# Token numbers inside the sorted rows, a fixed GpSimd issue order, and smaller edits in a fused attention and expert kernel

## The chip, the cores and the metric

The kernel runs on one core of a Trainium2 chip. Its time is the device time of one execution in microseconds (us), taken by the chip. A profiled execution also leaves a trace: what each engine did and when. The engines are PE (matrix products), DVE (vector), ACT (activation functions), POOL (GpSimd) and SP, which here only issues transfers. POOL issues the transfers that convert float32 to float16 and those that scatter rows to places given by an index list.

## The reference

Attention over 8 batches, 8 heads, 576 tokens and 64 columns a head, with a bias that a small two-layer network (MLP) computes from the distance of two tokens; then every token goes through the one expert, of eight, that its domain number names.

```python
scores = scale * np.matmul(q, k.transpose(0, 1, 3, 2))
psi_rel = np.log1p(np.abs(rel))                       # rel = i - j
psi_i = np.log1p(np.maximum(pos[:, None], 1.0))
h = np.maximum((psi_rel / psi_i)[..., None] @ w1 + b1, 0.0)   # 32 hidden
scores = scores + (h @ w2).transpose(2, 0, 1)[None]
attn = softmax(scores); x = attn @ v                  # -> x: 4608 tokens x 512
for e in range(8):
    mask = domain_id == e
    out[mask] = np.maximum(x[mask] @ w1[e], 0.0) @ w2[e]      # 512 -> 1024 -> 512
```

## The kernel before, in words

The program runs through these stages. PE, DVE and ACT execute in the order in which the code is written; on POOL and SP a scheduler of the compiler chooses the order.

**Setup** (L63 to L108). Number tables are made on POOL by sixteen iota instructions, four for each quarter of the partitions, and turned into two tables: L4 (logarithms of distances, 1711 columns) and slope (144 columns).

**Bias** (L111 to L164). Nine blocks `ib` of 64 queries. For each, 16 tiles `hr` (128 x 576, the hidden layer) are made on DVE (L126), PE multiplies them with W2BIG into PSUM tiles `eb` (L136, L141), and ACT writes the exponentials out as biasM, biasR, biasL and biasRL (L150 to L164). The last 64 keys are computed twice, once for each half of the partitions (L140).

**Zero fill**. x_dram (`fire_x`), 9984 rows of 512 float16, is filled with zeros by one transfer on SP (L694). On the same queue the second part of the domain numbers, `dom2` (L183), stands behind it.

**Route** (L167 to L292). DVE counts the tokens of each expert and computes `posi`, the row of each token in sorted order; one count goes through PE (`app`, L207), which stands behind the last bias product in PE's order. Then a second table in DRAM, `fire_perm`, is filled with a pad number, 40 scatters on POOL (L287, one for each column of 128 or 64 tokens) write every token's number of 4 bytes to its row, and one transfer on SP reads the table back as `sidx` (L292).

**Attention** (L295 to L536). For each batch: the loads of q, k and v on POOL (two batches ahead), transposes on PE, then 21 units of scores. A unit is two or more products on PE into `sc`, an exponential on ACT (L412, `e`), and a product with the bias on DVE (L417). The products with v (`av`) are spread between later units; `norm` (L454 to L473) divides by the row sums, and five scatters a batch on POOL (L477) send 4 x 128 and 64 rows of 1 KB to x_dram. For the last 64 queries the product with v runs on 64 columns of one head at a time (L439, L444) and `norm` writes the tile `xl`.

**Experts** (L547 to L614). x_dram is read back by SP, 640 rows for an expert (`xg`, L578), transposed on PE (L559), multiplied with w1e (L601), through a Relu on ACT (L605), multiplied with w2e (L566); DVE copies 128 rows at a time from PSUM to `res` (L569, four buffers), and POOL scatters these rows to the output by `sidx` (L570). The weights of experts 0 to 2 are loaded early into three buffers, those of 3 to 6 all at the start of this stage (L591 to L593), those of 7 when a buffer comes free.

Of the kernel before, what the change touches and what calls it, by code (L numbers as in the profile page):

```python
# [16 lines left out]
P = 128  # L17
S = 576
# [12 lines left out]
PAD = 1 << 20  # L31

# [23 lines left out]
def _no_order(tc, key, inst):  # L56

    ins = inst.ins if hasattr(inst, "ins") else inst
    tc.declare_no_dep(ins, group=key, reason="rows of one permutation")
    tc.add_to_no_dep_group(key, ins)  # L60


def _setup_constants(tc, G, w1, b1, w2):  # L63
# [12 lines left out]
    nc.sync.dma_start(out=w1col, in_=bass.AP(tensor=w1.tensor, offset=0, ap=[[0, 4], [1, 32], [1, 1]]))  # L76
    G.nb1 = cst.tile([P, 1], F32, tag="nb1", name="nb1")
    nc.sync.dma_start(out=G.nb1, in_=bass.AP(tensor=b1.tensor, offset=0, ap=[[0, 4], [1, 32], [1, 1]]))
    nc.vector.tensor_scalar(out=G.nb1, in0=G.nb1, scalar1=-1.0, scalar2=None, op0=AO.mult)
# [9 lines left out]
    si = cst.tile([P, NGR], I32, tag="si", name="si")  # L89
    li = G.tmp.tile([P, W4 + W1], I32, tag="li", name="li")  # L90
    for g in range(4):
        pg = slice(32 * g, 32 * g + 32)

        nc.gpsimd.iota(si[pg, 0:128], base=4 * g, channel_multiplier=0, pattern=[[1, 4], [16, 32]])
        nc.gpsimd.iota(si[pg, 128:144], base=512 + g, channel_multiplier=0, pattern=[[4, 16]])
        nc.gpsimd.iota(li[pg, 0:W4], base=-(C4 + 4 * g), channel_multiplier=0, pattern=[[1, W4]])
        nc.gpsimd.iota(li[pg, W4:], base=-(C1 + 512 + g), channel_multiplier=0, pattern=[[1, W1]])
    G.slope = cst.tile([P, NGR], F32, tag="slope", name="slope")
    nc.vector.tensor_copy(out=G.slope, in_=si)
    nc.vector.tensor_scalar(out=G.slope, in0=G.slope, scalar1=1.0, scalar2=None, op0=AO.max)  # L100
    nc.scalar.activation(out=G.slope, in_=G.slope, func=AF.Ln, bias=1.0, scale=1.0)
    nc.vector.reciprocal(out=G.slope, in_=G.slope)
    nc.vector.tensor_scalar(out=G.slope, in0=G.slope, scalar1=w1col[:], scalar2=None, op0=AO.mult)
    lf = G.tmp.tile([P, W4 + W1], F32, tag="lf", name="lf")
    nc.vector.tensor_copy(out=lf, in_=li)
# [190 lines left out]
class _Attention:  # L296
# [152 lines left out]
    def norm(self, b, p):  # L449
# [5 lines left out]
        if p < 4:  # L455
            if p == 0:
                self.xt[b] = asb.tile([P, 4, 512], F16, tag="xt", name="xt", bufs=2)
# [282 lines left out]
```

## Time and profile before

| | us |
|---|---|
| median of 3 runs | 527.84 |
| lowest, highest | 526.59, 532.48 |
| the profiled execution | 523.68 |
| its span in the trace | 522.0 |
| busy: PE, DVE, ACT, POOL | 373.6, 260.3, 231.1, 202.0 |

The span is what the trace covers; 1.7 us of the execution lie around it. No engine is busy for the whole span, so what bounds the kernel changes from stage to stage and is read stage by stage. In a line of the timeline the first number is the start, the second the length, and the bracket tells how long the engine had been idle and what ended that.

### The profile page before, as it was taken

The page shows a single profiled execution, that of the slowest core. Times are in us where ns is not written, and L with a number is a line of the kernel's source. Part 1 is how long each engine was busy: PE and PEld are TensorE (multiplying, and loading weights), DVE is VectorE, ACT ScalarE, POOL GpSimd, SP SyncE. Part 2 cuts the span into 40 slices and gives each one's busy share as a digit, 9 for nine tenths or more (in the row PEclk, how much of TensorE's full clock was granted, in tenths as well). Part 3 has the DMA queues.
Part 4 walks back from the last instruction along what each step waited for, and adds up shares of the span by engine and source line. Part 5 has one row for each costly group of instructions (what it writes and reads, how often), then busy time and mean ns, then how long its engine had stood idle before and what let it go on. Part 6 is the DMA issues. An engine that isn't in the chain of part 4 may idle for free. (4 is left out here: it accounts for less than half of the span.)

```text
span 522.0 us, 10886 instructions
## 1 busy us (share of the span) xinstructions
PE 373.6 (72%) x4578; PEld 235.3 (45%) x4578; DVE 260.3 (50%) x572; ACT 231.1 (44%) x290; POOL 202.0 (39%) x238
## 2 busy tenths in 40 slices
PE   0578844311298988889898977079639999999992
PEld 0366733100055555465555544055425566566550
DVE  5899985100369695777768674013022422422411
ACT  1444521000388987889697875021402143143140
POOL 9740445777606546543403042603013303313312
PEclk9999999555599999999897989579959999999997
DMA  0999987000992999979401010899998313102211
GB/s 3 155 233 366 319 123 131 2 0 0 99 155 53 161 203 149 151 124 114 77 3 46 4 46 21 160 241 241 215 246 206 112 50 123 69 22 88 81 39 73
DMA packets 79034, 61.39 MB, mean 118 GB/s; under 512 B 23558, under 2 KB 71430, under 8 KB 78984
## 3 DMA queue, kind: packets, MB, share of 16 engines
q0 software_dynamic: 56576, 45.12, 49.7%
q1 hardware_dynamic: 22408, 15.57, 10.8%
q8 instruction: 36, 0.59, 0.4%
q14 instruction: 14, 0.11, 0.1%
HBM read 67.17 MB, written 25.49 MB: 177 GB/s over the span
## 5 line engine op out<-in xcount | busy, mean ns | idle before, releaser
L412 ACT ACTIVATE e<-sc 128x1024 f16<-128x1024 f32 x168 | 156.7, 998 | 93.5 <-remote 67.2
L605 ACT ACTIVATE hT<-hps 128x640 f16<-128x640 f32 x64 | 45.1, 704 | 137.8 <-PE hps L601 136.2
L570 POOL DMA_INDIRECT out_dram<-res,sidx x40 | 39.5, 988 | 132.6 <-DVE res L569 131.9
L566 PE MATMUL ops<-w2e,hT 128*128 128x512 f16 x320 | 71.5, 383 | 0.0
L601 PE MATMUL hps<-xT,w1e 128*128 128x320 f16 x512 | 71.2, 300 | 0.0
L385 PE MATMUL sc<-qkT 64*128 64x512 f16 x256 | 54.3, 407 | 22.7 <-ACT e L412 16.7
L477 POOL DMA_INDIRECT fire_x<-xt,posi x32 | 34.4, 1076 | 81.2 <-DVE xt L459 71.0
L569 DVE COPY res<-ops 128x512 f32<-128x512 f32 x40 | 27.7, 691 | 76.2 <-PE ops L566 51.0
L417 DVE TENSOR_TENSOR e<-e,biasM 128x1024 f16<-128x1024 f16 x96 | 63.4, 685 | 3.3 <-ACT e L412 3.0
L601 PEld LDWEIGHTS <-w1e 128*128 128x128 f16 x512 | 50.3, 98 | 20.7
L136 PE MATMUL eb<-W2BIG,hr 128*128 128x32 f16 x576 | 36.0, 196 | 25.8 <-DVE hr L126 18.8
L433 PE MATMUL pu<-vext,e 128*128 128x65 f16 x1024 | 53.0, 199 | 0.0
L126 DVE TENSOR_SCALAR hr<-L,slope,nb 128x576 f16<-128x576 f16 x144 | 51.6, 435 | 1.7 <-ACT L L108 1.7
L561 DVE COPY xT<-pxt 128x512 f16<-128x512 f16 x40 | 15.8, 421 | 65.8 <-PE pxt L559 64.1
L566 PEld LDWEIGHTS <-hT 128*128 128x128 f16 x320 | 31.3, 99 | 36.8 <-issue 1.4
L287 POOL DMA_INDIRECT fire_perm<-nidx,posi x40 | 38.7, 969 | 21.0 <-issue 21.0
L433 PEld LDWEIGHTS <-e 128*128 128x128 f16 x1024 | 46.2, 102 | 0.0
L367 DVE COPY qkT<-pt 128x1024 f16<-128x1024 f16 x32 | 21.8, 683 | 47.7 <-remote 43.5
L136 PEld LDWEIGHTS <-hr 128*128 128x128 f16 x576 | 26.5, 117 | 34.7 <-DVE hr L126 17.6
L429 PE MATMUL pu<-vrag,e 128*128 128x130 f16 x128 | 29.9, 234 | 13.1 <-DVE xl L470 7.9
L559 PE MATMUL pxt<-idn,xg 128*128 128x128 f16 x160 | 15.1, 235 | 33.6 <-DMA xg<-fire_x 18.1
L345 PE MATMUL pt<-idn,qn 128*64 128x128 f16 x256 | 15.3, 249 | 27.1 <-DVE qkT L367 14.3
(123 smaller groups left out, 407.6 us busy)
## 6 DMA issues: line engine op xcount, KB each, us to landing
fire_x<-zero SPq DMA_DIRECT2D x1, 9984.0 KB, 37.0
w1e<-in_moe_w_dram POOLq DMA_DIRECT2D x8, 1024.0 KB
w2e<-in_moe_w_dram POOLq DMA_DIRECT2D x8, 1024.0 KB
xg<-fire_x SPq DMA_DIRECT2D x8, 640.0 KB, 8.6
qn<-in_q_dram POOLq DMA_DIRECT2D x8, 512.0 KB
kn<-in_k_dram POOLq DMA_DIRECT2D x8, 512.0 KB
vst<-in_v_dram POOLq DMA_DIRECT2D x8, 512.0 KB
fire_perm<-nidx,posi POOLq DMA_INDIRECT x40
```

The source lines that it names most:

```text
L126: nc.vector.tensor_scalar(out=hr, in0=G.L4[:, c0: c0 + S], scalar1=G.slope[:, m: m + 1], scalar2=G.nb1[:], op0=AO.mult, op1=AO.max)
L136: nc.tensor.matmul(out=eb[:, lj, 32 * k16: 32 * k16 + 32], lhsT=rap(hr, jc, [[4, 128]]), rhs=G.W2BIG[:, 0:32], start=True, stop=True)
L287: _no_order(tc, "slots", nc.gpsimd.indirect_dma_start(out=G.perm_dram[:, :], out_offset=bass.IndirectOffsetOnAxis(ap=G.posi[0:n, c:c + 1], ...
L385: mm(out=sc[:, h2, :], lhsT=self.qkT[b, p][hs[h2], 1, 128 * c: 128 * c + 128], rhs=self.qkT[b, p][hs[h2], 0, :], start=not raw, stop=True)
L412: nc.scalar.activation(out=ef[:, 0:n], in_=sf[:, 0:n], func=AF.Exp, bias=0.0, scale=0.125)
L417: self.nc.vector.tensor_tensor(out=job[0], in0=job[0], in1=job[1], op=AO.mult)
L433: mm(out=self.pu[:, c // 2, o + 65 * h2: o + 65 * h2 + 65], lhsT=self.e[b, ("m", p, j)][:, h2, 128 * c: 128 * c + 128], rhs=vx[:, 2 * p + ...
L477: _no_order(self.tc, "x_rows", self.nc.gpsimd.indirect_dma_start(out=self.x_dram[:, :], out_offset=bass.IndirectOffsetOnAxis(ap=self.G.pos ...
L566: nc.tensor.matmul(out=ops_, lhsT=hT[:, fc, t0: t0 + 128], rhs=w2e[:, fc, :], start=(fc == 0), stop=(fc == 7))
L570: _no_order(tc, "out_rows", nc.gpsimd.indirect_dma_start(out=out[:], out_offset=bass.IndirectOffsetOnAxis(ap=idx, axis=0), in_=res[:], in_ ...
L601: nc.tensor.matmul(out=hps[:, hf, 0:HC], lhsT=w1e[:, dc, 128 * fc: 128 * fc + 128], rhs=xT[:, dc, HC * hf: HC * hf + HC], start=(dc == 0), ...
L605: nc.scalar.activation(out=hT[:, fc, :].rearrange("p (a b) -> p a b", a=2), in_=hps[:, :, 0:HC], func=AF.Relu, bias=0.0, scale=1.0)
```

## The change

1. **Token numbers.** A row of x_dram grows from 512 to 514 float16 (`XW = DM + 2`, 1028 bytes): the last two hold the token's number as one int32. It is written into `xt` and `xl` by a small iota on POOL (`new_rows`), travels with the scatter of the rows, comes back with `xg`, and is the index of the output scatter. The table fire_perm, its pad transfer, its 40 scatters and `sidx` are gone. The pad number is written by the zero fill.
2. **Order on POOL.** An `_Issue` object puts each load, iota and weight load behind the one before it; scatters between two such instructions are free among themselves.
3. **Fetches of rows**: one transfer of 128 rows instead of 640, two experts ahead instead of three. **Weights** of expert e + 3 are issued behind the first output scatter of expert e. `res` has six buffers.
4. **Last queries**: 128 columns, two heads at once, in `av`; `norm` of `xl` in two pieces, `norm` of `xt` in one instruction instead of two.
5. **Bias**: of 16 hidden tiles, three (3, 8, 13) are made on ACT; the last keys are multiplied once; the setup has fewer and wider iotas, and a chain of small DVE operations and two absolute values on ACT in their place.

```diff
+XW = DM + 2
+class _Issue:
+    def __init__(self, tc):
+        self.tc, self.fixed, self.free = tc, None, []
+    def _behind(self, ins, before):
+        self.tc.add_manual_dep(ins, before.name, mybir.DependencyInfo(
+            mybir.DependencyClass.NoSync, mybir.DependencyReason.DATA), reason="issue order")
+    def __call__(self, inst):
+        ins = _ins(inst)
+        for before in self.free or ([self.fixed] if self.fixed is not None else []):
+            self._behind(ins, before)
+        self.fixed, self.free = ins, []
+        return inst
+    def scatter(self, inst):
+        ins = _ins(inst)
+        if self.fixed is not None:
+            self._behind(ins, self.fixed)
+        self.free.append(ins)
+        return inst
...
-                nc.vector.tensor_scalar(out=hr, in0=G.L4[:, c0: c0 + S],
-                                        scalar1=G.slope[:, m: m + 1], scalar2=G.nb1[:],
-                                        op0=AO.mult, op1=AO.max)
+                if k16 in (3, 8, 13):
+                    nc.scalar.activation(out=hr, in_=G.L4[:, c0: c0 + S], func=AF.Relu,
+                                         bias=G.pb1[:], scale=G.slope[:, m: m + 1])
+                else:
+                    nc.vector.tensor_scalar(out=hr, in0=G.L4[:, c0: c0 + S],
+                                            scalar1=G.slope[:, m: m + 1], scalar2=G.nb1[:],
+                                            op0=AO.mult, op1=AO.max)
...
-    for bb in range(B):
-        for t in range(NT):
-            n = 128 if t < 4 else 64
-            c = NT * bb + t
-            _no_order(tc, "slots", nc.gpsimd.indirect_dma_start(
-                out=G.perm_dram[:, :],
-                out_offset=bass.IndirectOffsetOnAxis(ap=G.posi[0:n, c:c + 1], axis=0),
-                in_=nidx[0:n, bb, t:t + 1], in_offset=None))
-    G.sidx = pbuf.tile([P, E * NCH, 1], I32, tag="sidx", name="sidx")
-    nc.sync.dma_start(out=G.sidx, in_=bass.AP(tensor=G.perm_dram.tensor, offset=0,
-                                              ap=[[1, 128], [128, E * NCH], [1, 1]]))
...
+            h2, q = c // 2, 2 * (c % 2)
             ex = self.e[b, ("x",)]
+            out = self.pu[:, h2, o: o + 130].rearrange("p (q d) -> p q d", q=2)
+            mm(out=out, lhsT=ex[:, 0, 64 * q: 64 * q + 128],
+               rhs=vr[:, q: q + 2, 65 * h2: 65 * h2 + 65], start=True, stop=False, skip_group_check=True)
+            for j in range(4):
+                l0 = 256 * (j % 2) + 64 * q
+                mm(out=out, lhsT=self.e[b, ("l", j // 2)][:, h2, l0: l0 + 128],
+                   rhs=vx[:, 2 * q + h2: 2 * q + h2 + 3: 2, j, :], start=False, stop=(j == 3),
+                   skip_group_check=True)
...
+    def new_rows(self, tag, n, c, base, step):
+        t = self.G.asb.tile([n, c, XW], F16, tag=tag, name=tag, bufs=2)
+        self.G.issue(self.nc.gpsimd.iota(t[:, :, DM:].bitcast(I32), base=base, channel_multiplier=step,
+                                         pattern=[[1, c], [0, 1]]))
+        return t
...
-        res = msb.tile([P, DM], F32, tag="res", name="res", bufs=4)
+        res = msb.tile([P, DM], F32, tag="res", name="res", bufs=6)
...
     def fetch(e):
-        xg = msb.tile([P, NCH, DM], F16, tag="xg", name="xg", bufs=3)
-        nc.sync.dma_start(out=xg, in_=x_dram[e * CAP: e * CAP + CAP, :]
-                          .rearrange("(k p) d -> p k d", p=128))
-        return xg
+        tiles = []
+        for kk in range(NCH):
+            xg = msb.tile([P, XW], F16, tag="xg", name="xg", bufs=4 * NCH)
+            r0 = e * CAP + 128 * kk
+            nc.sync.dma_start(out=xg, in_=x_dram[r0: r0 + 128, :])
+            tiles.append(xg)
+        return tiles
...
-        if e == 0:
-            for e2 in range(G.NW, min(E, G.NW + G.NW2)):
-                G.wts[e2] = _load_expert(nc, G.wsb2, moe_w1, moe_w2, e2, G.NW2)
...
         for kk in range(NCH):
-            second(hT, 128 * kk, w2e, G.sidx[:, e * NCH + kk, :])
-        if e + G.NW + G.NW2 < E:
-            G.wts[e + G.NW + G.NW2] = _load_expert(nc, G.wsb, moe_w1, moe_w2, e + G.NW + G.NW2, G.NW)
+            second(hT, 128 * kk, w2e, xgs[e][kk][:, DM:])
+            if kk == 0 and e + G.NW < E:
+                e2 = e + G.NW
+                pool, n = (G.wsb2, G.NW2) if e < G.NW2 else (G.wsb, G.NW)
+                G.wts[e2] = _load_expert(nc, pool, moe_w1, moe_w2, e2, n, G.issue)
```

On POOL, between the end of the routing's constants and the first scatter of attention rows, this stands before (qn, kn, ql, kl, vst and vrag are the loads of q, k and v; w1e and w2e those of an expert's weights):

```order
L337 DMA vrag_126<-in_v_dram 64x4x64 x2
L541 DMA w1e<-in_moe_w_dram 128x4x1024
L325 DMA ql<-in_q_dram 64x8x64
L325 DMA kl<-in_k_dram 64x8x64
L543 DMA w2e<-in_moe_w_dram 128x8x512
L541 DMA w1e<-in_moe_w_dram 128x4x1024
L287 DMA fire_perm<-nidx,posi 9984x1 x40
L323 DMA qn<-in_q_dram 128x8x256
L323 DMA kn<-in_k_dram 128x8x256
```

And this in the change:

```order
L297 MEMSET pb 128x672
L355 DMA qn<-in_q_dram 128x8x256
L358 DMA ql<-in_q_dram 64x8x64
L355 DMA kn<-in_k_dram 128x8x256
L358 DMA kl<-in_k_dram 64x8x64
L365 DMA vst<-in_v_dram 128x8x256
L372 DMA vrag_130<-in_v_dram 64x4x64 x2
L516 IOTA xt 128x4
```

The 40 scatters and the three weight loads ahead of them are gone from this place, and the loads for batches 2 and 3 stand where they were.

On POOL, at the change from attention to the experts, this stands before:

```order
L477 DMA fire_x<-xt,posi 9984x512 x4
L477 DMA fire_x<-xl,posi 9984x512
L541 DMA w1e<-in_moe_w_dram 128x4x1024
L543 DMA w2e<-in_moe_w_dram 128x8x512
L541 DMA w1e<-in_moe_w_dram 128x4x1024
L543 DMA w2e<-in_moe_w_dram 128x8x512
L541 DMA w1e<-in_moe_w_dram 128x4x1024
```

And this in the change:

```order
L522 DMA fire_x<-xt,posi 9984x514 x4
L516 IOTA xl 64x1
L522 DMA fire_x<-xl,posi 9984x514
L613 DMA out_dram<-res,xg 4608x512
L588 DMA w1e<-in_moe_w_dram 128x4x1024
L590 DMA w2e<-in_moe_w_dram 128x8x512
L613 DMA out_dram<-res,xg 4608x512 x5
```

The eight weight loads ahead of the first output scatter become one pair behind every fifth output scatter.

On ACT, in the bias stage, one block of 64 queries reads so in the change (before, the first of these rows is not there):

```order
L174 ACTIVATE hr<-L_108,pb_83,slope 128x576 x3
L203 ACTIVATE biasM<-eb 128x2x6x64
L206 ACTIVATE biasM<-eb 128x2x2x64
L203 ACTIVATE biasM<-eb 128x2x6x64
L206 ACTIVATE biasM<-eb 128x2x2x64
L200 ACTIVATE biasR<-eb 64x4x64 x2
```

ACT now makes three of a block's hidden tiles before it evacuates the block's products.

## Rows read from the trace of the kernel before

**Rows 1.** Windows by stage: length, each engine's busy time (instructions), PEclk, DMA share, GB/s

```profile
16.00:67.57 51.57, 41.89 (x798) 32.74 (x798) 51.57 (x145) 23.31 (x49) 21.03 (x25) 1.00 1.18 269
88.59:139.42 50.83, 8.86 (x72) 4.76 (x72) 4.28 (x8) 4.09 (x4) 37.01 (x39) 0.51 0.12 12
139.42:327.08 187.66, 160.53 (x2562) 98.17 (x2561) 137.30 (x284) 152.65 (x164) 71.96 (x77) 0.95 0.66 95
327.08:342.36 15.28, 0.00 (x1) 0.01 (x1) 0.00 (x1) 0.00 (x0) 7.89 (x10) 0.50 0.92 177
342.36:511.76 169.40, 153.94 (x992) 92.94 (x992) 42.63 (x79) 45.07 (x64) 40.04 (x41) 0.95 0.53 132
```

**Rows 2.** Timeline around the token number scatters: start, length, engine, line, what

```profile
82.87 1.05 POOL L287 DMA_INDIRECT fire_perm<-nidx,posi  x1 [9.15 <-issue]
...
132.60 0.90 POOL L287 DMA_INDIRECT fire_perm<-nidx,posi  x1 [0.30 <-issue]
...
139.38 0.69 DVE L367 COPY qkT<-pt 128x1024 f16<-128x1024 f16 x1 [26.07 <-remote]
139.42 4.87 ACT L412 ACTIVATE e<-sc 128x1024 f16<-128x1024 f32 x5 [22.19 <-remote]
```

**Rows 3.** Timeline beside the last batch's row scatters

```profile
323.80 0.42 PE L444 MATMUL pu<-vext,e 128*64 128x65 f16 x8
...
326.17 0.20 DVE L454 RECIPROCAL rz<-pu 64x8 f32<-64x8 f32 x1 [3.45 <-remote]
```

**Rows 4.** Timeline of setup's end and of one block of the bias stage

```profile
14.34 1.63 ACT L108 ACTIVATE L<-lf 128x1711 f16<-128x1711 f32 x1 [4.46 <-DVE lf L106]
...
16.00 44.13 DVE L126 TENSOR_SCALAR hr<-L,slope,nb 128x576 f16<-128x576 f16 x122 [1.70 <-ACT L L108]
...
46.18 0.81 ACT L153 ACTIVATE biasM<-eb 128x768 f16<-128x768 f32 x1 [2.71 <-PE eb L136]
...
51.64 0.81 ACT L153 ACTIVATE biasM<-eb 128x768 f16<-128x768 f32 x1 [2.70 <-PE eb L136]
...
53.64 0.77 ACT L150 ACTIVATE biasR<-eb 64x256 f16<-64x256 f32 x2
```

**Rows 5.** Groups by line: the wide iotas of setup, busy and mean ns

```profile
L96 POOL IOTA li<- 32x1075 int32 x4 | 4.1, 1021 | 0.0
L97 POOL IOTA li<- 32x636 int32 x4 | 2.6, 661 | 0.0
```

**Rows 6.** Transfers, KB each and us to landing: the zero fill

```profile
fire_x<-zero SPq DMA_DIRECT2D x1, 9984.0 KB, 37.0
```

**Rows 7.** Timeline: the zero fill's issue, the domain numbers behind it, the route's first step

```profile
27.35 0.65 SPq L694 DMA_DIRECT2D fire_x<-zero  x1
...
28.04 31.70 SPq L183 DMA_DIRECT2D dom<-in_moe_domain_id_dram  x1
...
67.57 0.17 DVE L187 CAST domf<-dom 128x40 f32<-128x40 int32 x1
```

**Rows 8.** Timeline at the change to the experts

```profile
330.31 15.26 SPq L578 DMA_DIRECT2D xg<-fire_x  x4
...
342.36 2.81 PE L559 MATMUL pxt<-idn,xg 128*128 128x128 f16 x20 [18.14 <-DMA xg<-fire_x]
```

**Rows 9.** Tile xg: all eight of its transfers

```profile
DMA to landing us min/median/max: 4.3/8.6/23.6
```

**Rows 10.** Timeline of the experts: the first product of experts 1, 2, 3, and DVE's wait

```profile
364.65 8.86 PE L601 MATMUL hps<-xT,w1e 128*128 128x320 f16 x64
...
385.21 0.69 DVE L569 COPY res<-ops 128x512 f32<-128x512 f32 x1 [21.39 <-DMA out_dram<-res,sidx]
...
397.52 8.86 PE L601 MATMUL hps<-xT,w1e 128*128 128x320 f16 x64
...
416.87 8.31 PE L601 MATMUL hps<-xT,w1e 128*128 128x320 f16 x60
```

**Rows 11.** The page's GB/s in 40 equal slices of 13.05 us

```profile
GB/s 3 155 233 366 319 123 131 2 0 0 99 155 53 161 203 149 151 124 114 77 3 46 4 46 21 160 241 241 215 246 206 112 50 123 69 22 88 81 39 73
```

More of the change, by code (lines that the diff above doesn't have):

```diff
@@ new lines, in _setup_constants @@
+    pi = cst.tile([P, 1], I32, tag="pi", name="pi")
+    nc.gpsimd.iota(pi, base=0, channel_multiplier=1, pattern=[[0, 1]])
+    li = G.tmp.tile([P, W4 + W1], I32, tag="li", name="li")
+    nc.gpsimd.iota(li[:, 0:W4], base=-C4, channel_multiplier=0, pattern=[[1, W4]])
+    nc.gpsimd.iota(li[:, W4:], base=-(C1 + 512), channel_multiplier=0, pattern=[[1, W1]])
+    si = cst.tile([P, NGR], I32, tag="si", name="si")
+    nc.gpsimd.iota(si[:, 0:128], base=0, channel_multiplier=0, pattern=[[1, 4], [16, 32]])
@@ new lines, in _setup_constants @@
+    nc.gpsimd.iota(si[:, 128:144], base=512, channel_multiplier=0, pattern=[[4, 16]])
+    pf = cst.tile([P, 2], F32, tag="pf", name="pf")
+    nc.vector.tensor_copy(out=pf[:, 0:1], in_=pi)
+    g1 = cst.tile([P, 1], F32, tag="g1", name="g1")
+    nc.vector.tensor_scalar(out=g1, in0=pf[:, 0:1], scalar1=32.0, scalar2=None, op0=AO.is_ge)
+    for lim in (64.0, 96.0):
+        nc.vector.tensor_scalar(out=pf[:, 1:2], in0=pf[:, 0:1], scalar1=lim, scalar2=None, op0=AO.is_ge)
+        nc.vector.tensor_tensor(out=g1, in0=g1, in1=pf[:, 1:2], op=AO.add)
@@ new lines, in _setup_constants @@
+    gs = cst.tile([P, 3], F32, tag="gs", name="gs")
+    nc.vector.tensor_scalar(out=gs[:, 0:1], in0=g1, scalar1=4.0, scalar2=None, op0=AO.mult)
+    nc.vector.tensor_scalar(out=gs[:, 1:2], in0=g1, scalar1=-4.0, scalar2=None, op0=AO.mult)
+    nc.vector.tensor_scalar(out=gs[:, 2:3], in0=g1, scalar1=-1.0, scalar2=None, op0=AO.mult)
+    lf = G.tmp.tile([P, W4 + W1], F32, tag="lf", name="lf")
+    G.L4 = cst.tile([P, W4 + W1], F16, tag="L4", name="L4")
+    nc.scalar.activation(out=lf[:, 0:W4], in_=li[:, 0:W4], func=AF.Abs, bias=gs[:, 1:2], scale=1.0)
@@ new lines, in _setup_constants @@
+    nc.scalar.activation(out=G.L4[:, 0:W4], in_=lf[:, 0:W4], func=AF.Ln, bias=1.0, scale=1.0)
+    G.slope = cst.tile([P, NGR], F32, tag="slope", name="slope")
+    nc.vector.tensor_scalar(out=G.slope[:, 0:128], in0=si[:, 0:128], scalar1=gs[:, 0:1], scalar2=1.0,
+                            op0=AO.add, op1=AO.max)
+    nc.vector.tensor_scalar(out=G.slope[:, 128:], in0=si[:, 128:], scalar1=g1[:], scalar2=1.0,
+                            op0=AO.add, op1=AO.max)
+    nc.scalar.activation(out=G.slope, in_=G.slope, func=AF.Ln, bias=1.0, scale=1.0)
@@ L88, in _setup_constants @@
         )
[L89 to L105, printed above, removed]
-    nc.vector.scalar_tensor_tensor(out=lf, in0=lf, scalar=-1.0, in1=lf, op0=AO.mult, op1=AO.max)
-    G.L4 = cst.tile([P, W4 + W1], F16, tag="L4", name="L4")
-    nc.scalar.activation(out=G.L4, in_=lf, func=AF.Ln, bias=1.0, scale=1.0)
+    nc.scalar.activation(out=lf[:, W4:], in_=li[:, W4:], func=AF.Abs, bias=gs[:, 2:3], scale=1.0)
+    nc.scalar.activation(out=G.L4[:, W4:], in_=lf[:, W4:], func=AF.Ln, bias=1.0, scale=1.0)
 def _phase_bias(tc, G):
@@ L139, in _phase_bias @@
                         else:
-                            for h2 in range(2):
-                                nc.tensor.matmul(
-                                    out=eb[64 * h2: 64 * h2 + 64, lj, 32 * k16: 32 * k16 + 32],
-                                    lhsT=hr[:, 512:576], rhs=G.W2BIG[:, 0:32], start=True, stop=True)
+                            nc.tensor.matmul(out=eb[0:64, lj, 32 * k16: 32 * k16 + 32],
+                                             lhsT=hr[:, 512:576],
+                                             rhs=G.W2BIG[:, 0:32], start=True, stop=True)
                 ebv = eb.rearrange("p l (i h) -> p l h i", h=8)
@@ L437, in av @@
         else:
+            h2, q = c // 2, 2 * (c % 2)
             ex = self.e[b, ("x",)]
-            mm(out=self.pu[0:64, c // 2, o: o + 130], lhsT=ex[:, 0, 64 * c: 64 * c + 64],
-               rhs=vr[:, c, :], start=True, stop=False, skip_group_check=True)
-            for h2 in range(2):
-                for j in range(4):
-                    l0 = 256 * (j % 2) + 64 * c
-                    mm(out=self.pu[0:64, c // 2, o + 65 * h2: o + 65 * h2 + 65],
-                       lhsT=self.e[b, ("l", j // 2)][:, h2, l0: l0 + 64],
-                       rhs=vx[:, 2 * c + h2, j, :], start=False, stop=(h2 == 1 and j == 3),
-                       skip_group_check=True)
+            out = self.pu[:, h2, o: o + 130].rearrange("p (q d) -> p q d", q=2)
```

134 lines of the change are left out of this document (68 added, 66 removed).

## The prediction

> **What bounds the kernel now.** I read the windows by stage first, because they show where the span goes; then the timeline at each stage in which every compute engine idles; then the waits that end there. In [rows 1] three stretches are poor. From 88.59 to 139.42 us, 50.83 us, ACT runs 4 instructions and PE is busy for 8.86 us; only POOL works. From 327.08 to 342.36 PE, DVE and ACT do nothing for 15.28 us. In the last stage, 169.40 us, PE is busy for 153.94 but ACT and DVE for under a third. The other stages are bound by one engine: DVE is busy for all 51.57 us of the bias stage, and ACT for 152.65 of the 187.66 us of attention (164 of its 8 x 21 = 168 units; four fell into the stretch before).
>
> The timeline of the first poor stretch [rows 2] starts and ends with the 40 scatters of token numbers on POOL: 82.87 to 133.50, one every 1.28 us (132.60 less 82.87, over 39). Only six microseconds after the last one do DVE and ACT go on, having waited 26.07 and 22.19 us for "remote". What they waited for is PE's signal that a tile is done. The same delay shows, smaller, beside the row scatters of the last batch [rows 3]: PE's last product into `pu` ends at 324.22 by the trace, DVE starts on it at 326.17, 1.95 us later, while five scatters run. So I read the stall as PE's signals (and its pace) suffering under back-to-back scatters. Which part of the chip delays them no row tells.
>
> **The change part by part.** The sum is made against the profiled execution: 523.68 us, its span of 522.0 and 1.7 around it. That lies 4.2 below the median and 2.9 below the lowest of the three runs.
>
> *Setup, 0.* Fewer iotas free POOL: three of four 1.02 and 0.66 us ones go [rows 5], 5.0 us. But DVE's and ACT's chain to the first `hr` now holds ten small DVE steps, a second table load on ACT and, in front of `hr`, the four W2BIG copies that used to stand ahead of it. By my count of the chain it ends where it did, at 16.00 [rows 4]; bounds -2 and +2. POOL's 5 us do count for the zero fill, which waits behind POOL's first loads: it should start near 22.4 instead of 27.35 [rows 7].
>
> *Bias, -5.0.* DVE makes 122 tiles in 44.13 us, 0.362 each; a block of 16 takes 51.64 less 46.18 = 5.46 late in the stage [rows 4], and 51.57 / 9 = 5.73 in the mean, since the first blocks are slower. With 13 tiles DVE takes 4.7. ACT now has the block's evacuation, from 51.64 to 53.64 + 0.77 = 54.41, so 2.77, and three Relu of 128 x 576. No row shows one. The ends are 0.38, half of the 0.77 for two of 256 columns, and the 0.81 of 768 columns; between them 576 columns come to 0.65, which I take (the Ln of 1711 columns in 1.63 gives 0.55 by columns alone): 1.95 for three. Between ACT's last tile and its next evacuation stand a signal, PE's products and another signal: I allow 0.45, between 0 and the 2.70 that ACT idles there now. Together 5.17 a block, so ACT replaces DVE as the bound: 9 x (5.73 - 5.17) = 5.0. Bounds: -9 (4.7 a block) and -1. The route gains from it only if its domain numbers are there, see the first rival. The halved products for the last keys lie beside this on PE, 41.89 busy of 51.57, and count nothing.
>
> *The 40 scatters, -48.4.* POOL is free after the head's transposes, and the loads for batches 2 and 3 go out there at once. The route and the head stay: 21.02 us from 67.57 to 88.59, less some 2.1 for the first unit's late signal (a delay of the size in [rows 3]). The 50.83 us go, except for the four units made in it: at attention's pace, 187.66 / 164 = 1.14 each, 4.6 us. So -46.3 - 2.1. Bounds: nothing, if the stall has another cause (a rival), and -50.8.
>
> *Attention otherwise, 0.* One instruction instead of two per `norm` of xt saves DVE little, `xl` in two pieces costs about as much; ACT's 152.65 us cover both. The 128-column blocks stream the same columns: 4 x 5 products of 130 where 4 x (1 x 130 + 8 x 65) were. If that cover were gone it would be some tenths a batch. The new iotas on POOL (8 x 2, a small fraction of a microsecond by [rows 5]) stand behind the weight loads and must be there before DVE writes xt; that is a wait that did not exist, priced below. Range -8 to +8.
>
> *To the experts, -8.3.* SP issues the fetch at 330.31 and PE starts at 342.36, 12.05 us later [rows 8], while eight weight loads share the transfer engines. The quickest of the eight xg transfers landed in 4.3 us [rows 9], with 640 rows; now the first 128 rows suffice and no weights stand there. I take 3.7, a little under the quickest, between 2.2 (half of it, for a fifth of the bytes) and 8.6 (the median). Bounds -10 and -3.5.
>
> *The experts, -13.5.* Expert 1 begins at 364.65, expert 2 at 397.52, expert 3 at 416.87 [rows 10]: a period of 32.87 against 19.35. The difference, 13.5, is PE held up behind DVE, which waits 21.39 us for a `res` buffer whose scatter stands in the queue behind eight weight loads. With one pair of loads per expert and six buffers that wait should go. What is late next is the same scatter behind one pair: see the third rival. Bounds -13.5 and 0.
>
> Sum: -5.0 - 48.4 - 8.3 - 13.5 = -75.2, so **448.5** for an execution like the profiled one. The runs lie above it, so I predict **450**.
>
> **The rivals.**
>
> *The zero fill becomes the bound.* It lands at 27.35 + 37.0 = 64.35 [rows 6, 7], and `dom2` stands behind it: SP needs 31.70 us to issue that transfer. DVE's first route step at 67.57 comes just after. In the change DVE wants it 5.0 earlier, at 62.6; a fill from 22.4 lands at 59.4 if it keeps its speed. But each packet is now 1028 bytes at a stride of 1028, no longer on round boundaries. Every microsecond past 62.6 is lost whole, as the head's copies stand behind the route on DVE. At 1.25 times the 37.0 it lands at 68.7: +6, **456**; at 1.5 times at 77.9: +15, 465. For it: the gap is 3 us wide. Against: the fill holds 366 GB/s [rows 11] with 1 KB packets, and 4 bytes more are 0.4%. The Trainium skill speaks against the change here ("DMA: Bandwidth & Descriptors", section "How a descriptor splits into AXI transactions"): transactions start at multiples of 256 bytes, so a descriptor that does not start there costs extra beats of 32 bytes. By that rule I estimate 33 to 40 beats a row instead of 32, about 1.14 times, which would give 42 us and a landing near 64.6, so 452; no row here shows it. Chance of a loss over 3 us by the fill: 0.17.
>
> *The fill makes it slower than before.* The same place, another size: if unaligned rows cost the fill over three times its time (partial rows read, merged and rewritten), it lands at 22.4 + 3.3 x 37.0 = 144, DVE stands at the route until then for 82 us, and the 75 are eaten: about **531**. It decides from a factor of 3.2. Nothing in the rows shows such a factor. Chance 0.02.
>
> *Transfers crowd.* A batch now brings, by the tile shapes, 1.7 MB of q, k and v, 0.6 MB of scattered rows and, in three batches, 2.1 MB of weights: 4.4 MB in the 23.5 us of a batch, 187 GB/s. An expert brings 2.1 MB of weights, 1.3 of output, 0.7 of rows, 4.1 in 19.35, 210 GB/s. The rows show 177 in the crowded gap [rows 1] and 160 to 246 in the slices from 326 to 404 us [rows 11]. So it fits, with a tenth to spare. At 177 an expert's transfers would need 23.0 us, 3.6 late in each of five experts, and a batch 24.9: +18 and +4, less what six `res` buffers and the loads' lead of a batch absorb. I give **460** (450 + 10) a chance of 0.18. POOL's fixed order makes this worse, since the iota of xt waits behind any load that waits.
>
> *The stall stays.* If the 50.8 us do not come from the scatters but from something in the first batch's start, only POOL's time goes: 448.5 + 46, about **495**. Against it: stall and scatters begin and end together, and [rows 3] shows the delay again beside scatters. That the change doesn't do what it says has the same result. Chance 0.04.
>
> *Better than the sum.* Attention's 1.14 us a unit stand above ACT's busy 152.65 / 164 = 0.93. If half a tenth of that comes back (168 x 0.05 = 8) and bias runs at DVE's 4.7 (another 4): 450 - 12 = **438** or less. Chance 0.06.
>
> **How the numbers follow.** Forecast 450, with its own spread 441 to 457: 0.52. Fill late 0.17, crowding 0.18, stall stays 0.04, better 0.06, slower 0.02, no change 0.01. The range 438 to 472 takes in the forecast, the fill up to 1.5 times, crowding up to +22 and half of "better", and leaves out about 0.15. A change of under 1% can't be told from none here. Faster by over 1%: 0.97; within 1%: 0.01; slower: 0.02.
>
> **What would show it.** In the new profile: no idle stretch of ACT between the first unit (about 81.5 us) and the end of attention near 274; the route's first step on DVE waiting for nothing or for `dom2` (then the first rival); ACT without idle time in the late bias blocks and a period of about 5.2 us; 5 to 8 us from the last `xl` to the first transposes; expert periods of 19.35 with no wait of DVE for output scatters. The prediction is wrong if attention stalls again beside loads or weights, or if DVE waits for the domain numbers.

## The result and the profile after

The changed kernel takes **463.69 us** (median of 4 runs, 462.45 to 464.15) where the kernel before takes 527.22 beside it (4 runs, 524.74 to 532.48): ratio 0.878, 95% interval 0.871 to 0.8849. The forecast was 450 with a range of 438 to 472. So the sign and the range hold; the point is 13.7 us too low. The profiled execution took 463.56, span 462.0, so the spans fell by 60.0 where the sum said 75.2.

The windows by stage of the changed kernel show where. Columns are as in [rows 1]: the stretch, its length, and the busy time of PE, PEld, DVE, ACT and POOL, granted clock, DMA share, GB/s.

```profile
14.25:67.03 52.78, 35.23 (x720) 30.81 (x721) 41.67 (x117) 45.68 (x79) 5.95 (x13) 1.00 1.23 195
67.03:85.72 18.69, 0.00 (x0) 0.03 (x1) 1.41 (x5) 0.79 (x3) 0.00 (x0) 1.00 0.86 135
102.17:288.57 186.40, 159.62 (x2516) 96.72 (x2514) 142.49 (x275) 155.61 (x168) 80.52 (x99) 0.99 0.77 116
288.57:296.62 8.05, 0.00 (x1) 0.01 (x1) 0.00 (x1) 0.00 (x0) 3.28 (x5) 0.65 0.31 92
296.62:453.32 156.70, 153.03 (x992) 92.17 (x992) 42.66 (x79) 45.07 (x64) 47.58 (x49) 0.99 0.70 157
```

Two stretches of [rows 1] have changed their character. The 50.83 us in which only POOL worked are gone: all 168 units of attention lie in one stretch of 186.40 us, with ACT busy for 155.61. And a new empty stretch stands where there was none: from 67.03 to 85.72 PE does nothing, DVE and ACT are busy for 1.41 and 0.79 us, and transfers run. The timeline of the changed kernel says what they are (start, length, engine, line, what, and in the bracket the idle time before it and what ended that):

```profile
20.76 0.64 SPq L739 DMA_DIRECT2D fire_x<-zero  x1
21.45 51.26 SPq L232 DMA_DIRECT2D dom<-in_moe_domain_id_dram  x1
...
84.16 0.19 DVE L236 CAST domf<-dom 128x40 f32<-128x40 int32 x1 [25.65 <-DMA dom<-in_moe_domain_id_dram]
...
85.72 0.19 PE L256 MATMUL app<-rowtot,ut 128*128 128x8 f16 x2 [18.69 <-DVE rowtot L248]
...
102.17 2.85 ACT L447 ACTIVATE e<-sc 128x1024 f16<-128x1024 f32 x3 [34.33 <-PE sc L426]
```

Read beside [rows 7], this is the first rival. The zero fill starts 6.6 us earlier (20.76 for 27.35), but SP now needs 51.26 us instead of 31.70 to issue what stands behind it, and the domain numbers are there only at 84.16. DVE waits 25.65 us for them, and PE, which finished its bias products at 67.03, waits 18.69 for DVE.

The bias block in the changed kernel, for [rows 4]:

```profile
36.36 0.81 ACT L203 ACTIVATE biasM<-eb 128x768 f16<-128x768 f32 x1 [0.47 <-PE eb L187]
...
39.14 2.38 ACT L174 ACTIVATE hr<-L,pb,slope 128x576 f16<-128x576 f16 x3
41.99 0.81 ACT L203 ACTIVATE biasM<-eb 128x768 f16<-128x768 f32 x1 [0.47 <-PE eb L187]
```

ACT is idle for 0.47 us in a block and for no more: it is the bound. The three Relu take 2.38, 0.79 each, and the period is 41.99 - 36.36 = 5.63.

The change to the experts and the experts' periods, for [rows 8 to 10]: a timeline, then the landing times of tile xg, then one line of the waits (line, what it waited for: total, times, longest).

```profile
294.44 5.58 SPq L624 DMA_DIRECT2D xg<-fire_x  x12
...
296.62 0.61 PE L602 MATMUL pxt<-idn,xg 128*128 128x128 f16 x4 [9.43 <-DMA xg<-fire_x]
...
319.74 8.86 PE L644 MATMUL hps<-xT,w1e 128*128 128x320 f16 x64
...
339.09 1.11 PE L644 MATMUL hps<-xT,w1e 128*128 128x320 f16 x7
```

```profile
DMA to landing us min/median/max: 2.1/2.9/3.4
```

```profile
DVE res L612 <- PE ops L609: 52.0, 40, 9.7
```

PE starts 2.2 us after SP's fetch, and experts 1 and 2 begin 19.35 apart, the good period of [rows 10]. All 40 waits for `res` end with PE: none is left for a scatter of outputs.

### The profile page after: what moved, and what is told of

Its sections match the earlier page's. It is cut to its first block, busy times and chain, and to the rows that moved or that the text cites. A ratio compares the mean times of both kernels' runs of the same rounds, so it can differ in the third digit from the quotient of the medians.

```text
span 462.0 us, 10318 instructions
## 1 busy us (share of the span) xinstructions
PE 353.6 (77%) x4306; PEld 224.1 (48%) x4306; DVE 247.3 (54%) x536; ACT 254.7 (55%) x321; POOL 152.5 (33%) x201
## 5 line engine op out<-in xcount | busy, mean ns | idle before, releaser
L613 POOL DMA_INDIRECT out_dram<-res,xg x40 | 40.0, 1000 | 113.7 <-DVE res L612 106.9
L420 PE MATMUL sc<-qkT 64*128 64x512 f16 x256 | 50.6, 390 | 8.6 <-ACT e L447 8.6
L187 PE MATMUL eb<-W2BIG,hr 128*128 128x32 f16 x576 | 26.9, 194 | 31.4 <-ACT hr L174 15.4
L469 PE MATMUL pu<-vext,e 128*128 128x65 f16 x1024 | 50.9, 195 | 0.0
L469 PEld LDWEIGHTS <-e 128*128 128x128 f16 x1024 | 44.1, 99 | 0.1
L177 DVE TENSOR_SCALAR hr<-L,slope,nb 128x576 f16<-128x576 f16 x117 | 41.7, 437 | 2.6 <-PE eb L191 2.6
L187 PEld LDWEIGHTS <-hr 128*128 128x128 f16 x576 | 22.3, 116 | 35.4 <-ACT hr L174 17.9
L355 POOL DMA_DIRECT2D qn<-in_q_dram x8 | 7.4, 925 | 83.8 <-PE pt L380 83.8
L420 PEld LDWEIGHTS <-qkT 64*128 64x128 f16 x256 | 13.7, 93 | 31.9 <-issue 25.1
L465 PEld LDWEIGHTS <-e 128*128 128x128 f16 x128 | 12.4, 97 | 32.9 <-issue 19.6
```

Source lines behind the costliest of these rows:

```text
L177: nc.vector.tensor_scalar(out=hr, in0=G.L4[:, c0: c0 + S], scalar1=G.slope[:, m: m + 1], scalar2=G.nb1[:], op0=AO.mult, op1=AO.max)
L187: nc.tensor.matmul(out=eb[:, lj, 32 * k16: 32 * k16 + 32], lhsT=rap(hr, jc, [[4, 128]]), rhs=G.W2BIG[:, 0:32], start=True, stop=True)
L420: mm(out=sc[:, h2, :], lhsT=self.qkT[b, p][hs[h2], 1, 128 * c: 128 * c + 128], rhs=self.qkT[b, p][hs[h2], 0, :], start=not raw, stop=True)
L465: mm(out=self.pu[:, c // 2, o: o + 130], lhsT=er[:, p % 2, 128 * c: 128 * c + 128], rhs=vr[:, p, :], start=True, stop=False, skip_group_ch ...
L469: mm(out=self.pu[:, c // 2, o + 65 * h2: o + 65 * h2 + 65], lhsT=self.e[b, ("m", p, j)][:, h2, 128 * c: 128 * c + 128], rhs=vx[:, 2 * p + ...
L613: inst = nc.gpsimd.indirect_dma_start(out=out[:], out_offset=bass.IndirectOffsetOnAxis(ap=idx.bitcast(I32), axis=0), in_=res[:], in_offset ...
```

## The experiments

Twelve kernels were run, four each on three chips; those with a ratio below ran four times, the others once. The chips matter: beside the first two sets the kernel before took 497.56 and 497.86 us (7 runs each), beside the third 525.57, as in the runs of the prediction. So a number below is compared with its own set, or stage by stage.

**1. The fill: order or speed?** The first set takes the wait away in two ways, and then asks what makes the fill slow. Domain numbers first, their memset and two loads taken out of the route into a function that is called ahead of the fill:

```diff
+            _load_domains(nc, G, moe_domain_id)
             zero = G.cst.tile([P, 1, XW], F16, tag="zero", name="zero")
```

> The two loads of the domain numbers are issued ahead of the zero fill instead of behind it; the fill is unchanged. Theory (the domain numbers stand behind a fill that has become slow): the 25.65 us that VectorE waits for them at 84.16 go, TensorE's 18.69 us at app go with them, and the time falls from 463.6 by 18.7 to about 445. The fill still lands near 83, ahead of the first scatter of rows near 108 minus 19 = 89. Rival (something else holds the start of the attention as well: q, k and v arriving late under the fill, or the first scatter waiting for the fill): app starts at 67, but the first exponential does not come 16.5 us behind it, and less than 10 us are gained, 454 or more.

Measured 440.25 us (ratio 0.8842, 0.8811 to 0.8873). The timeline:

```profile
59.11 0.17 DVE L242 CAST domf<-dom 128x40 f32<-128x40 int32 x1
...
67.64 0.21 PE L262 MATMUL app<-rowtot,ut 128*128 128x8 f16 x2
...
83.89 2.86 ACT L453 ACTIVATE e<-sc 128x1024 f16<-128x1024 f32 x3 [15.38 <-PE sc L432]
```

DVE waits for nothing at `domf`, `app` follows PE's last bias product without a gap, and the first exponential comes 16.25 later (16.45 in the changed kernel). The fill is as slow as ever (it lands 59.4 us after its issue) and costs little now: 1 us against the fast fill below. Then the fill itself, with the order left as in the change:

```diff
-            zero = G.cst.tile([P, 1, XW], F16, tag="zero", name="zero")
-            nc.gpsimd.memset(zero[:, :, 0:DM], 0.0)
-            nc.gpsimd.memset(zero[:, :, DM:].bitcast(I32), PAD)
-            nc.sync.dma_start(out=x_dram.rearrange("(p c) d -> p c d", p=P), ...)
+            zero = G.cst.tile([P, 1, 512], F16, tag="zero", name="zero")
+            nc.gpsimd.memset(zero.bitcast(I32), PAD)
+            nc.sync.dma_start(out=bass.AP(tensor=x_dram.tensor, offset=0,
+                                          ap=[[40448, P], [512, 79], [1, 512]]), ...)
```

The padding number, read as two half-precision values, is zero and a number near zero, so padded rows may hold it in every column. The next two runs use the same edit with `offset=2` and with pieces of 544 elements.

> The fill writes the same region as pieces of 1024 bytes, each at a multiple of 1024 bytes, all of them the padding number; the rows, their length of 1028 bytes and everything else are unchanged, and the domain numbers still stand behind the fill. Theory (the fill is slow because of its 1028-byte pieces): while it runs alone it moves about 380 GB/s as before the change, not 180; the domain numbers land near 50 to 60 instead of 84, and the time is about 445. Rival (the fill is slow for what runs beside it, or for the time at which it starts): the rate stays near 180 GB/s and the time near 463.

> As the fill in pieces of 1024 bytes, but every piece starts 4 bytes behind a multiple of 1024. If where a piece starts and ends is what costs (it cuts a line of the memory at both ends): about 180 GB/s and 463 us, as with rows of 1028 bytes. If the length over 1024 bytes is what costs: about 380 GB/s and 445 us.

> The fill in pieces of 1088 bytes, each at a multiple of 64 bytes. If a length over 1024 bytes is what costs, or an end that is no multiple of 512 bytes: about 190 GB/s (1088/1028 of 180) and 460 to 463 us. If an end inside 64 bytes is what costs: about 380 GB/s and 445 us.

Measured 439.20 us (ratio 0.8821, 0.8788 to 0.8853), 466.65 and 438.80 (one run each). The window from 40 to 52 us, when little else moves, in the changed kernel, in pieces of 1024 bytes, in the same pieces 4 bytes on, and in pieces of 1088 (last column GB/s):

```profile
40.00:52.00 12.00, 7.64 (x163) 6.83 (x164) 11.09 (x34) 10.54 (x20) 0.00 (x0) 1.00 1.12 187
```

```profile
40.00:52.00 12.00, 7.86 (x171) 7.00 (x172) 10.98 (x33) 10.98 (x20) 0.00 (x0) 1.00 1.09 385
```

```profile
40.00:52.00 12.00, 7.52 (x160) 6.69 (x160) 10.92 (x33) 9.44 (x17) 0.00 (x0) 1.00 1.12 157
```

```profile
40.00:52.00 12.00, 7.89 (x170) 7.01 (x170) 10.93 (x33) 10.98 (x20) 0.00 (x0) 1.00 1.12 350
```

And from issue to landing in the last three:

```profile
fire_x<-zero SPq DMA_DIRECT2D x1, 10112.0 KB, 36.7
```

```profile
fire_x<-zero SPq DMA_DIRECT2D x1, 10112.0 KB, 70.6
```

```profile
fire_x<-zero SPq DMA_DIRECT2D x1, 10064.0 KB, 39.0
```

So neither the 4 bytes more nor a length over 1024 is what costs. 1024 bytes that start 4 bytes off take 70.6 us, 1088 bytes at multiples of 64 take 39.0. Where a piece starts and ends, counted from the start of the table, halves the rate. The runs show multiples of 64 bytes to be fast and of 4 to be slow; 16 and 32 were not tried. The Trainium skill ("Collectives: The Full Stack", section "Rules for kernel authors") asks for buffers of collectives aligned to 32 bytes, since the hardware otherwise reads, modifies and writes. That agrees with these rates, but no row here shows the reading.

**2. The stall: the scatters, or GpSimd?** The prediction held that PE's signals suffer under back-to-back scatters. On the kernel with the aligned fill, the 40 scatters were put back, or GpSimd was kept busy without any transfer; the changed kernel and the kernel before ran beside them.

```diff
     nc.vector.tensor_copy(out=G.posi, in_=posf)
+    for bb in range(B):
+        for t in range(NT):
+            ...
+            inst = nc.gpsimd.indirect_dma_start(out=perm_dram[:, :], ..., in_=nidx[0:n, bb, t:t + 1], in_offset=None)
+            G.issue(inst)
```

```diff
     nc.vector.tensor_copy(out=G.posi, in_=posf)
+    G.issue(nc.gpsimd.tensor_copy(out=busy[:, 0:NCOL], in_=G.posi))
+    for i in range(130):
+        G.issue(nc.gpsimd.iota(busy, base=i, channel_multiplier=1, pattern=[[1, 256]]))
```

> On the kernel with the fill in pieces of 1024 bytes (439.2 us): the 40 scatters of token numbers are put back on GpSimd behind the route, into a table that nobody reads; the rows still carry their numbers. Theory (PE's signals and pace suffer under back-to-back scatters): in the 50 us of the scatters PE's granted clock falls and ACT makes a handful of units, as before the change, and 20 to 46 us come back, 459 to 485. Rival (the scatters only keep GpSimd, and what follows its late loads waits): the same time is lost with any other work of that length on GpSimd, see the run with GpSimd kept busy. Second rival (the scatters cost nothing by themselves, the stall came from the sums that were removed with them): about 440.

> On the same kernel (439.2 us): at the place of the scatters GpSimd is kept for about 50 us by 130 iotas of 128 x 256, and sends no transfer meanwhile. Theory (it is the scatters that hold PE's signals): attention goes on beside them; the loads of batch 2 come 50 us later, but two batches of 23.5 us are loaded already, so at most some 5 us are lost: 439 to 445. Rival (GpSimd being late is what costs): the same 20 us or more as with the scatters, 459 or more.

> The changed kernel as it is, a second time beside the others. Theory (the 18.7 us of the domain wait are all that the late fill costs, and the 4.7 us by which the two mended kernels lie under 463.7 - 18.7 = 445 come from what differs between two sets of runs): about 458.5. Rival (the slow fill costs another 5 us elsewhere in the kernel): about 463.

> The kernel before as it is, with a profile of its own: in the runs beside the last kernels it took 497.6 us with a mean granted clock of 0.925, in the runs shown 527.8 with 0.896. Theory (the stall at the 40 scatters has no fixed length): the stretch of 50.8 us without ACT is some 30 us shorter here and all other stages are as they were. Rival: the stall is as long, and another stage is shorter.

Measured: scatters back **478.72**, GpSimd busy **478.73**, the changed kernel 455.79 (ratio 0.9147, 0.9125 to 0.9169), the kernel before 497.73. Scatters and iotas cost the same, so on this chip it is not the scatters but GpSimd's time, and the expectation from "signals suffer" falls here. The timelines with scatters, then with iotas:

```profile
130.62 0.97 POOL L369 DMA_DIRECT2D qn<-in_q_dram  x1
...
137.37 0.39 PE L394 MATMUL ptl<-idn,ql 64*128 64x64 f16 x4 [31.85 <-DMA ql<-in_q_dram]
```

```profile
78.83 54.12 POOL L329 IOTA busy<- 128x256 int32 x130
133.09 0.91 POOL L359 DMA_DIRECT2D qn<-in_q_dram  x1
...
139.59 0.39 PE L384 MATMUL ptl<-idn,ql 64*128 64x64 f16 x4 [32.62 <-DMA ql<-in_q_dram]
```

The loads of batch 2 stand in GpSimd's queue behind the scatters or the iotas. Two batches are loaded ahead, but PE transposes a batch's q and k while the batch before it is scored, so it wants batch 2 near 106 us, one batch after the start and not two. It then waits for `ql` until 137.37 and 139.59. The kernel before shows the same on this chip; first its waits, then its timeline:

```profile
PE pt L345 <- DMA qn<-in_q_dram: 31.0, 1, 31.0
PE pt L345 <- DMA kn<-in_k_dram: 2.8, 1, 2.8
```

```profile
107.75 2.86 ACT L412 ACTIVATE e<-sc 128x1024 f16<-128x1024 f32 x3 [0.65 <-PE sc L391]
145.12 1.02 ACT L412 ACTIVATE e<-sc 128x1024 f16<-128x1024 f32 x1 [34.51 <-PE sc L385]
```

Beside the same scatters ACT here makes one unit after the other up to 110.6, where the ACT of [rows 2] made four up to 117 and waited for "remote". PE's pace, which the prediction put in brackets, is slow in that trace too. From 114.81 to 129.37 it makes six products one by one, and before each it is idle for 1.20 to 2.92 us on nothing that the profile shows ("issue"):

```profile
119.70 0.26 PE L345 MATMUL pt<-idn,kn 128*64 128x128 f16 x1 [2.54 <-issue]
122.50 0.26 PE L345 MATMUL pt<-idn,kn 128*64 128x128 f16 x1 [2.54 <-issue]
```

So the kernel before loses time at the scatters in two ways: through the late loads, which this chip shows alone, and in the profile of the prediction through PE's late products and signals, beside which attention came too late to wait for those loads. The 18.7 us of the domain wait are nearly all that the slow fill costs. On this chip the changed kernel waits 16.27 us for the domain numbers, and the aligned fill in the first set, on a chip where the kernel before takes the same time, is 455.79 - 439.20 = 16.6 faster.

**3. How long may GpSimd be busy?** The same edit with 65 iotas, in the third set.

> As the kernel with GpSimd kept busy, with 65 iotas instead of 130, 27 us instead of 54.1. Theory (what costs is that GpSimd issues the loads of batch 2 late: PE's transposes of batch 2 want them near 107 us, so the cost is GpSimd's time less a lead; 130 iotas took 54.1 us and cost 478.7 - 439.2 = 39.5, which gives a lead of 14.6): 27 - 14.6 = 12.5 us come back, 452, with PE waiting some 9 us for ql. Rival (GpSimd's work slows the other engines while it runs, in proportion): 19.8 us, 459. Second rival (two batches are loaded ahead, so nothing is lost before 47 us): 439 to 441.

Measured 459.47 us.

```profile
78.83 27.43 POOL L329 IOTA busy<- 128x256 int32 x65
106.40 0.91 POOL L359 DMA_DIRECT2D qn<-in_q_dram  x1
...
112.75 0.39 PE L384 MATMUL ptl<-idn,ql 64*128 64x64 f16 x4 [7.43 <-DMA ql<-in_q_dram]
116.85 0.39 PE L384 MATMUL ptl<-idn,kl 64*128 64x64 f16 x4 [3.71 <-DMA kl<-in_k_dram]
```

The 452 was expected from 439.2, a time of another chip. Within the set, attention (first exponential to the start of the last `xl`) takes 201.7 us, 185.2 in the kernel with two Relu tiles below: 16.5 more, between the 12.5 of a lead and the 19.8 of a share. The rows decide for the lead: PE waits 7.43 + 3.71 = 11.1 for the two loads, and until then ACT runs at its usual pace (24 units up to 106.7 us). The other 5.4 us are lost in the units that follow. Loads and scatters now crowd there, and PE's granted clock, the third number from the end, has fallen while PE waited:

```profile
78.80:106.00 27.20, 23.26 (x360) 14.30 (x359) 20.44 (x37) 21.65 (x24) 22.81 (x65) 1.00 0.01 2
106.00:130.00 24.00, 11.10 (x130) 6.78 (x131) 10.26 (x20) 7.91 (x9) 17.33 (x24) 0.71 1.29 170
```

It is 0.50 (1.2 GHz) from 112 to 122 us, where the kernel with two Relu tiles keeps 1.00 (2.4 GHz). How the 5.4 us divide between the two was not tried. By its 525.57 us for the kernel before, this chip should have the stall of [rows 2], though no profile of that kernel was taken on it, and it shows no late signal beside iotas. If so, a busy GpSimd alone does not delay PE. Putting the scatters back on such a chip was not run.

**4. The weights.** Third set: loads issued as before the change, with the six `res` buffers kept.

```diff
     for e in range(E):
+        if e == 0:
+            for e2 in range(G.NW, min(E, G.NW + G.NW2)):
+                G.wts[e2] = _load_expert(nc, G.wsb2, moe_w1, moe_w2, e2, G.NW2, G.issue)
...
-            if kk == 0 and e + G.NW < E:
-                ...
+        if e + G.NW + G.NW2 < E:
+            e2 = e + G.NW + G.NW2
+            G.wts[e2] = _load_expert(nc, G.wsb, moe_w1, moe_w2, e2, G.NW, G.issue)
```

> On the kernel with the fill in pieces of 1024 bytes (439.2 us): the weights of experts 3 to 6 are issued together at the start of expert 0 and those of expert 7 behind it, as before the change, instead of one pair per expert; the six res buffers stay. Theory (the output scatters stand behind eight weight loads): VectorE waits again for a res buffer, some 18 us at one place, and 10 to 13.5 us come back, 449 to 453. Rival (the six buffers alone take the wait away): no such wait, 439 to 441.

Measured 458.0 us, where 449 to 453 was expected from another chip's 439.2. From the last `xl` to the end it takes 188.3 us, where the next kernel, on the same chip with the change's loads, takes 173.3: **15.0** lost. The timeline of PE, and a line of DVE's waits:

```profile
281.65 0.61 PE L602 MATMUL pxt<-idn,xg 128*128 128x128 f16 x4 [14.41 <-DMA xg<-fire_x]
...
308.38 8.86 PE L647 MATMUL hps<-xT,w1e 128*128 128x320 f16 x64
...
332.81 8.86 PE L647 MATMUL hps<-xT,w1e 128*128 128x320 f16 x64
```

```profile
DVE res L612 <- DMA out_dram<-res,xg: 5.2, 1, 5.2
```

The loss has three main parts: 5.0 in front of the experts (13.46 for 8.44 us, xg landing beside eight weight loads), 4.1 in expert 0 (26.73 for 22.60 us: PE waits for each later xg too, 2.8 us in all, and its first products take 10.59 us for 9.51), and 24.43 - 19.35 = 5.1 between experts 1 and 2, where DVE waits 5.2 for a scatter and not the 18 expected. The last 0.8 lie behind PE's last product. So the spread loads are worth these 15.0 us. Without them the wait is still only a quarter of the 21.39 in [rows 10]: the rest of the change took most of it away. That the six buffers do this, and not the smaller fetches, was not tried apart, as no run has four buffers.

**5. A better version.** Fill aligned and domain numbers first, and ScalarE makes two of 16 tiles:

```diff
-                if k16 in (3, 8, 13):
+                if k16 in (5, 10):
```

> Fill in pieces of 1024 bytes, domain numbers issued ahead of it, and ScalarE makes two of the 16 hr tiles of a bias block (5 and 10) instead of three, VectorE 14. Theory (ScalarE sets the bias block: 2.77 of evacuation, three times 0.79, and 0.47): a block takes 2.77 + 2 x 0.79 + 0.47 = 4.82 on ScalarE and 14 x 0.345 = 4.83 on VectorE, against 5.63; 9 x 0.8 = 7 less, 432. Rival (the wait for PE's products grows as the tiles come later): a period of 5.3 or more, 436 to 440.

Measured **441.31 us** (439.18 to 442.82), ratio 0.8402 (0.8366 to 0.8437), so it beats both kernels: the changed one took 463.69 beside a kernel before of 527.22, this one beside 525.57. ACT, then DVE:

```profile
50.94 0.81 ACT L203 ACTIVATE biasM<-eb 128x768 f16<-128x768 f32 x1 [0.66 <-PE eb L187]
...
53.72 1.63 ACT L174 ACTIVATE hr<-L,pb,slope 128x576 f16<-128x576 f16 x2
...
56.01 0.81 ACT L203 ACTIVATE biasM<-eb 128x768 f16<-128x768 f32 x1 [0.66 <-PE eb L187]
```

```profile
14.25 44.34 DVE L177 TENSOR_SCALAR hr<-L,slope,nb 128x576 f16<-128x576 f16 x126
```

The period is 5.07, not 4.82, and ACT is still the bound. DVE needs 14 x 0.352 = 4.93 a block and is done with its tiles at 58.59, while PE waits for ACT's tiles up to the last block:

```profile
59.72 0.50 PE L187 MATMUL eb<-W2BIG,hr 128*128 128x32 f16 x10 [1.31 <-ACT hr L174]
```

ACT's block is 2.78 of evacuation, 1.63 for two Relu and 0.66 of idle time, where 0.47 was expected: its last tile is now 10 and no longer 13, so PE has the products of six tiles to make before ACT goes on, and not of three. PE's last bias product ends at 63.01, 3.3 earlier than with three tiles (by the traces; the two were not timed side by side), where 7 were expected: nine periods of 0.56 less are 5.0, and the first blocks, in which PE waits for DVE's tiles too, give 1.7 back. The transposes of batch 0 ahead of most of the route were tried on top:

```diff
     cnt = apref[:, 1, :, :]
+    yield
...
-            _phase_route(tc, G, moe_domain_id)
-            at.head()
+            route = _phase_route(tc, G, moe_domain_id)
+            next(route)
+            at.head()
+            for _ in route: pass
```

> As the kernel with two tiles on ScalarE, and the transposes of the first batch stand in VectorE's and PE's order behind the first part of the route (domf to apref) instead of behind all of it. Theory (the 16.4 us from app to the first exponential are VectorE's route, which the scores don't need): the first exponential comes some 6 to 7 us behind app instead of 16.4, and ScalarE runs ahead into the 16 e buffers while VectorE does the rest of the route: 423 to 428. Rival (VectorE is then late with the weights of the units, and ScalarE waits later for what it gained): the first exponential comes early, but the end of attention does not, 430 to 433.

Measured 443.92 us (ratio 0.8437, 0.8403 to 0.847), no faster. ACT and PE in its timeline:

```profile
67.53 2.86 ACT L454 ACTIVATE e<-sc 128x1024 f16<-128x1024 f32 x3 [3.75 <-PE sc L433]
83.40 1.02 ACT L454 ACTIVATE e<-sc 128x1024 f16<-128x1024 f32 x1 [13.01 <-PE sc L427]
```

```profile
81.75 0.64 PE L387 MATMUL pt<-idn,qn 128*64 128x128 f16 x8 [12.18 <-DVE qkTl L409]
```

Attention starts over 10 us earlier, makes three units and stops for 13.01: PE's next work in its written order is batch 1's transposes, whose copies stand on DVE behind the route. Attention ends 4.6 us later than without the edit (the last `xl` starts at 268.88 for 264.31). The 16 free `e` buffers help nobody while PE is held.

## Why the prediction was right, and where it was off

**Direction and range: right.** The stall and the wait for output scatters went, and the gap to the experts shrank, as the sum said. That the range held is in part luck. The fill cost 18.8 us, more than the 15 at its worst in the forecast, and by the prediction's own sign, DVE waiting for the domain numbers, the account is wrong there; 5.8 us that attention gained beyond the sum hid a part of it. The size also holds for this kind of chip only: beside a kernel before of 497.86 the same change gains 42.1 us, and not the 63.5 of the result.

**Setup and bias, -5.0: 2.1 too much.** The first `hr` starts at 14.25 rather than 16.00, inside the bound. ACT does replace DVE as the bound, but the Relu takes 0.79, not the 0.65 taken between 0.38 and 0.81: I interpolated by columns between rows of 256 and 768, and the upper end was right. That makes the period 5.63 instead of 5.17. PE's bias products end at 67.03 instead of 69.94.

**The zero fill, taken at its old speed: this is what failed.** I gave 0.17 to a late fill, at 1.25 to 1.5 times its length. It lasted at most 84.16 - 20.76 = 63.4 us, 1.7 times the 37.0 of [rows 6] (1.6 and 1.9 times in two of the experiments), and the 18.7 us are more than the whole miss. The step that failed is "4 bytes more are 0.4%": I priced bytes, and what costs is that every row starts and ends off a boundary. By the rule of the Trainium skill that I set beside it ("DMA: Bandwidth & Descriptors", section "How a descriptor splits into AXI transactions") it would have been an estimated 1.14 times. The trace shows more. If the table starts at a multiple of 256, a piece of 1024 bytes that starts 4 bytes off has by that rule 33 beats for 32, an estimated 1.03 times, where 70.6 us against 36.7 are 1.9: the rule does not account for what costs here. It does fit the pieces of 1088 bytes, which have 37 beats for 34 in the mean, an estimated 1.09 times, where 385 against 350 GB/s are 1.10.

**The scatters, -48.4: the size right, the cause half right.** Attention as a whole (first exponential to the end of the last `xl`) went from 238.49 to 186.40 us, 52.1 less, where 46.3 was set. The delay of PE that I read in [rows 2] is in that trace, in its own products as in its signals, but the kernel before is without it on another chip. What I missed shows there: the loads of batch 2, late behind 40 scatters, worth 31 + 2.8 us on PE. I had looked for no other cost of a busy GpSimd, and in the expectations still counted two batches of lead where the transposes leave one. With that cause alone the change gains 42.1 us (497.86 to 455.79). Why the remaining 5.8 us more were gained was not tried apart; ACT's idle time in the stage fell from 35.0 to 30.8.

**To the experts, -8.3: -7.2.** xg lands in 2.1 to 3.4 us, better than the 3.7 taken, but SP issues it 5.9 us after the last `xl` instead of 3.2, because the last five scatters of rows run until 292.75.

**The experts, -13.5: -12.7.** As worked out, with the period of 19.35; the 0.8 short of the sum are in expert 0 (23.12 us to the first product of expert 1, 22.29 before). The runs show what the single pairs are worth, not what six buffers are.

**What balances.** Span -60.0 against -75.2: the fill +18.8, bias +2.1, to the experts +1.1, experts +0.8, the stretch from `app` to the first exponential -0.2, attention -5.8, and the tail behind the last product, which I left alone, -1.6: together 15.2.

**The rivals.** Crowding did not show as a wait: nothing in the experts waits for weights, at 157 GB/s. "The stall stays" is out. Of "slower" the place was right, at half the factor it needed; that rows are read and merged no row shows. Of "better" attention came in, with its 5.8 us, and the bias did not.

## What to carry to other kernels

A row that grows by a few bytes is priced by where its ends fall, not by its length: keep the pitch of rows in memory at a multiple of 64 bytes, or fill the table in pieces that lie on such boundaries whatever the rows are (the second was tried here; scatters and fetches of such rows were not). What stands behind a large transfer on its queue inherits its length, so a small load that gates a stage is issued first. When a queue is held for 50 us, ask which load behind it is wanted first and when, and count the lead from the first instruction that reads it, not from the number of buffers.

## What the hardware showed that was not expected

- Writes to memory in pieces that start 4 bytes off, or at steps of 1028 bytes, run at 157 to 197 GB/s; pieces at multiples of 64 bytes at 350 to 385, in the same window of the bias stage.
- The same kernel before takes 497.6 and 497.9 us on two chips and 525.6 on a third, each within 1% over 7 runs. Of the 25.9 us between the spans profiled (522.0 in the profile of the prediction, 496.1 on the second chip), 25.1 lie in attention with the stretch at the 40 scatters (238.49 and 213.41). Without these scatters attention, to the start of the last `xl`, also takes longer where the kernel before is slower: 186.0, 185.2 and 185.4 us, against 180.7 to 181.1. Which part delays PE there stays open.
- A wait of PE can cost clock as well, and does not always. After 11.1 us of waits in the run with 65 iotas PE worked at a granted clock of 0.50 (1.2 GHz); after 31.85 us in the run with the scatters put back it was 0.50 from 137.4 to 145 us and 0.85 in the 10 us after that. In the changed kernel PE did nothing for 18.69 us behind the bias stage, and the clock stayed at 1.00 (2.4 GHz) there and in the work that followed. Why that wait was spared no run tells.
